# Three output projections as 64-row tiles, two blocks of tokens side by side

## The chip, the cores and the metric

The kernel runs on one core of a Trainium2 chip. The metric is device time in microseconds (us), lower is better. Engines: PE is TensorE (PEld its weight loads), DVE is VectorE, ACT is ScalarE, POOL is GpSimd, SP is SyncE, which here issues all DMAs.

## The reference

One transformer block in float32 on 2048 tokens of width 448: attention with 16 query heads of 28 and one key and value head, then a gated feed-forward of width 1792, each behind a layer norm and with a residual.

```python
x = A_x
h = x + _A_ref(_layernorm(x, axis=-1), A_wq, A_wk, A_wv, A_wo)
h2 = h + _B_ref(_layernorm(h, axis=-1), B_w1, B_w3, B_w2)
return h2
```

`_A_ref` ends with `o @ wo`, where `o` is the 2048 x 448 attention output and `wo` is 448 x 448. This last product is what the change touches.

## The kernel before

**Precision.** A float32 operand is split into a high part (float32r, 0) and a low part (1); a product is high x high + high x low + low x high. The attention output of a tile, transposed, is held as `OS[0]` and `OS[1]`, the weight as `WO[0]` and `WO[1]`. The 448 inputs are three chunks of 128 rows and one of 64. Both 64-row halves of chunk 3 of `OS` hold the same rows; in `WO[0]` rows 0 to 63 of chunk 3 are the high part and rows 64 to 127 the low part, so that one 128-row product gives two terms. A block of 128 tokens thus takes 3 x 3 + 2 = 11 matmuls (`mm_D`).

**Tiling.** The tokens are four tiles (t) of 512, each of four blocks (n) of 128. The attention of a tile is four groups of four heads (`NG`), a group 16 steps of 128 keys. A step is: scores transposed in three 32-row matmuls a head (L407), an exponential on ACT (L414), and the values product of all four heads (L423). Beside them, for groups that come later, run the score matmuls that find each row's maximum (L323, "units"), reduced on DVE (L333, L351) or by way of ACT (L344, L358, L364).

**Order.** All queues are written out by hand. The list `EVERY` sets the order of score matmuls (`H`), units (`U`, `D`, `S`, `E`, `R`) and values (`pv1`) on TensorE; it repeats every four steps. Other work is tied to a step: `at(s, fn)` puts `fn` into the instruction streams when step s is reached. Each engine takes its instructions in the order in which they are written; waits between engines are semaphores, put in where data or a buffer require it.

**The projection.** After step 14 of the first group of the next tile, the output of the tile that is done is projected: `wo_rows(t, n)` (11 full matmuls into one bank, then an add to the residual `X[t]` on DVE, L476) for n = 0 to 3. This happens for tiles 0, 1 and 2 within the attention; tile 3 is projected early in the feed-forward, in the same way. Between the blocks' projections stands other work on the same step: the layer norm statistics of blocks 0 to 2 (`ln_stats`: L195 and L196 on DVE), and in the stages of tiles 1 and 2 two normalizations of tile 0 (`ln_norm`: L211 on ACT) with their transposes and DMAs (`blocks`: L225 on DVE, L231 on SP). In the stages of tiles 1 and 2 the statistics of one earlier block stand ahead of the first projection.

**Banks.** PSUM has eight banks. One holds the values product, seven are dealt out by `bank()`, which takes the bank that a model of the engines (`Clock`) expects to be free first; `done()` gives it back.

**Half mode.** The feed-forward already has a scheme for 64-row tiles: `two` writes two lists of matmuls by turns, one on rows 0 to 63 and one on rows 64 to 127, into two banks; then the halves change banks. Before they do, `settle`, a one-element ACT read of one of the banks (L1028), orders the two halves' writes to a bank.

Of the kernel before, what the change touches and what calls it, by code (L numbers as in the profile page):

```python
# [10 lines left out]
AF = mybir.ActivationFunctionType  # L11
ALU = mybir.AluOpType
# [4 lines left out]
P = 128  # L17
S = 2048
D = 448
# [5 lines left out]
NQ = T // P  # L25
# [10 lines left out]
def block_kernel(  # L36
# [13 lines left out]
    ve, se, ge, pe, sy = nc.vector, nc.scalar, nc.gpsimd, nc.tensor, nc.sync  # L50
# [4 lines left out]
    def f(ap):  # L55
        return ap.bitcast(F32)
# [10 lines left out]
    X = [keep.tile([P, NQ, D], F32, name=f"X{t}") for t in range(NT)]  # L67
    ident = keep.tile([P, P], F32, name="ident")
    NEG = [keep.tile([P, 32], F32R, name=f"neg{k}") for k in range(2)]
    pexp = keep.tile([P, 32], F32, name="pexp")  # L70
# [3 lines left out]
    WO = [keep.tile([P, NG, D], F32R, name=f"WO{k}", tag=f"wo{k}") for k in range(2)]  # L74
    OT = keep.tile([P, NG, T], F32, name="OT")
    OS = [keep.tile([P, NG, T], F32R, name=f"OS{k}", tag=f"os{k}") for k in range(2)]
# [7 lines left out]
    def qs_tile():  # L84
        k, n_qs[0] = homes[n_qs[0] % len(homes)], n_qs[0] + 1
        return keep.tile([P, 2, T], F32R, name="qs", tag=f"q{k}")
# [52 lines left out]
    clock, ready = Clock(), {}  # L139
# [3 lines left out]
    def bank(name="pb"):  # L143
        k = min(free, key=lambda k: order[k])
        free.remove(k)
        if k < 7:
            ps = ps_w.tile([P, T], F32, name=name, tag=f"bank{k}")
        else:
            ps = ps_o.tile([P, T], F32, name="po")
        used[id(ps)] = ps, k  # L150
        ready.pop(id(ps), None)
        return ps

    def done(ps, at=None):
        k = used.pop(id(ps))[1]
        order[k] = ready.get(id(ps), clock.end) + 0.7 if at is None else at
        free.append(k)
# [155 lines left out]
    class Unit:  # L313
# [22 lines left out]
        def plain(self):  # L336
            self.ps = self.mm()
            self.red()
# [133 lines left out]
    def wo_rows(t, n):  # L472
# [3 lines left out]
        ve.tensor_tensor(X[t][:, n], ps, X[t][:, n], op=ALU.add)  # L476
        done(po)

    def split_w(k):
        wh, wl = [qs_tile().rearrange("p a (c m e) -> p (a c) m e", c=2, m=2)  # L480
                  for b in range(2)]
        ve.tensor_copy(wh, W13[k])
        ge.tensor_tensor(wl, W13[k], f(wh), op=ALU.subtract)
        return wh, wl
# [25 lines left out]
    with tc.tile_pool(name="start", bufs=1) as sp:  # L510
# [37 lines left out]
        def split_wo(c):  # L548
            ge.tensor_copy(WO[0][:, c], wo_r[:, c])
            r, k = (slice(0, P), 1) if c < 3 else (slice(64, P), 0)  # L550
            ge.tensor_tensor(WO[k][r, c], wo_r[r, c], f(WO[0][r, c]), op=ALU.subtract)

        def stats(t, *ns):
            for n in ns:
                ln_stats(t, n)
# [51 lines left out]
        def diffs(i, kt, n):  # L607
            us = HV[i, kt, n] = [[Unit(i, 2 * h + k, n, kt) for k in range(2)] for h in range(2)]
            return [(both_diff, u) for u in us]

        def sums(i, kt, n):
            return [(both_sum, u) for u in HV.pop((i, kt, n))]
# [4 lines left out]
        first = plain(0, 0, 0) + plain(0, 0, 1) + diffs(0, 0, 2) + plain(0, 1, 1) + sums(0, 0, 2) + plain(0, 1, 0) + diffs(0, 0, 3) + sums(0, 0, 3) + diffs(1, 0, 0) + sums(1, 0, 0) + plain(0, 2, 0) + plain(0, 2, 2) + plain(0, 2, 1) + plain(0, 3, 2) + plain(0, 3, 0) + diffs(0, 2, 3) + sums(0, 2, 3) + plain(0, 3, 1) + [(max_done, 0)] + diffs(1, 2, 0) + [(max_rows, 0), (max_out, 0)] + sums(1, 2, 0)  # L617
# [212 lines left out]
    def at(s, fn, *args):  # L830
        todo.setdefault(s, []).append((fn, args))

    for g in range(NG):
        at(1 + 2 * g, split_wo, g)
# [3 lines left out]
    for i in range(NI - 1):  # L838
        e = NC * (i + 1)
# [3 lines left out]
    for t in range(NT - 1):  # L843
        e = NC * NG * (t + 1)


        if t == 1:
            at(e + 14.7, ln_stats, 0, NQ - 1)
            at(e + 14.7, ln_rstd, 0)
        for n in range(NQ):  # L850
            at(e + 14.7, wo_rows, t, n)
            for m in {(1, 1): (0,), (1, 2): (1,), (2, 0): (2, 3)}.get((t, n), ()):
                at(e + 14.7, ln_norm, 0, m, True)
                at(e + 14.7, blocks, 0, m)
            if t == 0 and n == NQ - 1:
                continue
            late = NC * NG * (t + 2) + 14 if t < 2 else LAST - 12
            at(e + 14.7 if n < NQ - 1 else late + 0.7, ln_stats, t, n)
        if t:
            at(late + 2, ln_rstd, t)  # L860
            if t == 2:
                at(e + 18, fetch, 0)
# [15 lines left out]
    for s in range(AHEAD, LAST):  # L878
        i, c = divmod(s, NC)
        n, kt = divmod(c, NQ)  # L880
# [7 lines left out]
    units = [0] + [64 - 4 * (AHEAD - NC)] + [64] * (NI - 2)  # L888
# [98 lines left out]
    while n_pv[0] < LAST:  # L987
        for x in "H2 H0 H2 H1 H3 H0 H2 H1 H0 H3 H2 H0 H3 H1 H2 pv1 H2 H0 H1 H3 H2 H0 H1 H3 H2 H0 H1 H3 pv1 H2 H3 H1 H0 H2 H3 H1 H0 H2 H3 H1 H0 pv1 H1 H0 H2 H3 H1 H0 H3 H1 pv1 H3".split():
            if x != "pv1":
                score(int(x[1]))  # L990
                continue
            s = n_pv[0] + LAG
            if not values():
                continue
            if n_pv[0] in (LAST - 5, LAST - 2):
                WH[0, (n_pv[0] - LAST + 5) // 3] = split_w((n_pv[0] - LAST + 5) // 3)
            if n_pv[0] == LAST - 1:
                WS[0, 0] = split_w2(0)
            run(s + 0.4)
            run(s + 0.5)  # L1000
            run(s + 0.7)
            run(s)
# [8 lines left out]
    free.append(7)  # L1011
    order[7] = clock.end + 4

    HALF = (slice(0, 64), slice(64, 128))
    PAIRS3 = ((0, 0), (1, 0), (0, 1))
    FULL = 4
    def put_xd(t):
        XD[t] = wk_pool.tile([P, T], F32R, name="rb")
        se.activation(XD[t][:64], f(XT[t][2][64:, 3]), AF.Copy)

    def two(pairs):
        for units in zip(*pairs):
            for h, (ps, lhs, rhs, first, last) in enumerate(units):
                pe.matmul(ps[:, : rhs.shape[-1]], lhs, rhs, start=bool(first), stop=bool(last), skip_group_check=True)  # L1024
                clock.mm("half", h, ps, 0.016 + rhs.shape[-1] / 2400, first)

    def settle(ps):
        se.activation(pexp[:1, 8:9], ps[:1, :1], AF.Copy)  # L1028

    def hidden(t, k, ps, then=None):  # L1030
        sg = f(pt_ring()[:, 0])
# [17 lines left out]
    def products(t, W, m, h):  # L1049
        r = HALF[h]  # L1050
        u = [(W[b][r, c, 1 - m], XT[t][a][r, c]) for a, b in PAIRS3 for c in range(3)]
        return u + [(W[0][r, 3, 1 - m], XT[t][2][r, 3])]

    def ffn1_half(t, k, W, ps, late):
        us = [products(t, W, late, 0), products(t, W, 1 - late, 1)]
        if not late:
            us[0].append((W[1][HALF[0], 3, 1], XD[t][HALF[0]]))
            us[1].append((W[1][HALF[1], 3, 0], XT[t][2][HALF[1], 3]))
        to = (ps[0], ps[1]) if not late else (ps[1], ps[0])
        two([[(to[h], *u, not late and x == 0, late and x == len(us[h]) - 1) for x, u in enumerate(us[h])]  # L1060
             for h in range(2)])
        if not late:
            settle(ps[1])

    def ffn2(t, k, n):
        if n == 0 and k == 0:
            Y[t] = [bank() for _ in range(NQ)]
        hid, w2s = HID[t, k], WS[t, k]
        for m, (a, b) in enumerate(PAIRS3):
            pe.matmul(Y[t][n][:, :D], hid[a][:, n * P : (n + 1) * P], w2s[:, b],  # L1070
                      start=(k == 0 and m == 0), stop=(k == NF - 1 and m == 2), skip_group_check=True)

    def ffn2_half(t, k, late):
        if k == 0 and not late:
            Y[t] = [bank() for _ in range(NQ)]
        hid, w2s = HID[t, k], WS[t, k]
        us = [[], []]
        for h in range(2):
            for n0 in (2, 0) if late else (0, 2):
                n, r = n0 + (h ^ late), HALF[h]  # L1080
                for m, (a, b) in enumerate(PAIRS3):
                    us[h].append((Y[t][n], hid[a][r, n * P : (n + 1) * P], w2s[r, b],
                                  not late and k == 0 and m == 0, late and k == NF - 1 and m == 2))
        two(us)
        settle(Y[t][0 if late else 3])
# [47 lines left out]
    for t in range(NT):  # L1133
        for k in range(NF):
            end = t == tl and k >= NF - 2
            t2, k2 = divmod(NF * t + k + 2, NF)
            if t2 < NT:
                WH[t2, k2] = split_w(k2)
# [7 lines left out]
            else:  # L1146
                ps = [bank("pa"), bank("pa")]
# [54 lines left out]
```

## Time and profile before

| | us |
|---|---|
| median of 3 runs | 1160.41 (1159.94 to 1161.62) |
| the profiled execution, its own time | 1160.38 |
| its span | 1158.6 |
| projection of tile 0 (44 matmuls), start to the next score matmul | 280.36 to 289.65 |
| projection of tile 1 | 448.35 to 457.45 |
| projection of tile 2 | 615.89 to 625.00 |

Start times are from the first instruction of the span. A busy PE overlaps matmuls and isn't PE at its peak. In the timeline a row is a run of like instructions: start, length, engine, line, operation, output<-input, shapes, count, and in brackets the idle time before it with what ended it. The granted TensorE clock was 1.00 over the whole span. From about 30 to 738 us it is the attention, then the feed-forward.

### The profile page before, as it was taken

To read this page: it belongs to the slowest core of one execution; us is meant where nothing else is said; L and a number is where in the kernel's file an instruction comes from. 1 tells how busy PE (TensorE), PEld (TensorE's weight loads), DVE (VectorE), ACT (ScalarE), POOL (GpSimd) and SP (SyncE) were. 2 spreads that over 40 slices of the span, in tenths; PEclk is the share of its full clock that TensorE was granted. 3 is DMA by queue.
4 is the path that set the end of the run, shared out by engine and by line. 5 is a ranking of instruction groups with operands and counts; after the bars stand their busy time and mean duration, and the time that the engine had idled before them with its cause. 6 is when DMAs were issued, how large, how long until landed. Compare 5 with 4: busy or idle time off the path is not lost.

```text
span 1158.6 us, 25640 instructions
## 1 busy us (share of the span) xinstructions
PE 1149.0 (99%) x10154; PEld 772.7 (67%) x10154; DVE 805.8 (70%) x1498; ACT 764.3 (66%) x1587; POOL 330.2 (29%) x242
## 2 busy tenths in 40 slices
PE   8999999999999999999999999999999999999998
PEld 6664444446444445444445444589999999999997
DVE  8878999897999998999988983163543444344333
ACT  5649999997999997999997999512222222222221
POOL 5312001101101111110111011345565556556552
PEclk9999999999999999999999999999999999999999
DMA  4010100001000002000012100143211101000000
GB/s 168 10 38 1 34 13 18 19 15 47 19 12 10 19 24 54 19 20 3 19 24 55 50 19 14 56 103 96 73 39 20 41 1 49 17 33 33 1 1 33
DMA packets 66680, 38.15 MB, mean 33 GB/s; under 512 B 41728, under 2 KB 59392, under 8 KB 66560
## 3 DMA queue, kind: packets, MB, share of 16 engines
q1 hardware_dynamic: 66560, 36.51, 11.5%
q8 instruction: 79, 1.29, 0.5%
q14 instruction: 41, 0.34, 0.1%
HBM read 24.04 MB, written 7.47 MB: 27 GB/s over the span
## 4 chain that ended last, share of the span: by engine, by line
PE 94%; ACT 2%; DVE 2%; issue 1%; DMA 1%; SPq 0%; POOL 0%; ACTq 0%; POOLq 0%
PE po L423 21%; PE pb L407 20%; PE pa L1024 18%; PE pa L323 10%; PE pb L1024 9%; PE pa L166 5%; PE pb L166 4%; PE po L1024 4%; PE pb L1070 1%; ACT OT L430 1%; ACT ab L344 1%; DVE mx L333 1%; PE pb L273 0%; ACT pt L414 0%; PE po L166 0%
## 5 line engine op out<-in xcount | busy, mean ns | idle before, releaser
L333 DVE TENSOR_REDUCE mx<-pa 128x1 f32<-128x512 f32 x689 | 440.1, 685 | 22.1 <-PE pb L407 13.0
L407 PE MATMUL pb<-qs,KS 32*128 32x512 f32 x3072 | 384.9, 425 | 0.0
L414 ACT ACTIVATE pt<-pb 128x512 f32<-128x512 f32 x684 | 365.9, 621 | 20.1 <-PE pb L407 17.3
L407 PEld LDWEIGHTS pb<-qs,KS 32*128 32x128 f32 x3072 | 234.0, 182 | 132.2 <-ACT pt L414 66.9
L323 PE MATMUL pa<-KS,qs 32*128 32x512 f32 x886 | 311.7, 459 | 1.3
L1024 PE MATMUL pa<-xl,qs 64*128 64x512 f32 x1044 | 195.4, 388 | 0.0
L323 PEld LDWEIGHTS pa<-KS,qs 32*128 32x128 f32 x886 | 138.6, 182 | 83.6 <-DVE mx L333 46.3
L423 PE MATMUL po<-pt,VA 128*32 128x512 f32 x1368 | 182.2, 605 | 0.4 <-ACT pt L414 0.4
L1024 PE MATMUL pa<-xh,qs 64*128 64x512 f32 x739 | 159.9, 388 | 0.0
L454 POOL TENSOR_TENSOR OT<-OT,rb 128x512 f32<-128x512 f32 x15 | 19.7, 1311 | 458.1 <-DMA rb<-sd 240.9
L1024 PE MATMUL pb<-w2s,pt 64*128 64x448 f32 x1050 | 145.2, 360 | 0.0
L1034 DVE TENSOR_TENSOR pt<-pa,pt 128x512 f32<-128x512 f32 x49 | 33.8, 691 | 159.0 <-ACT pt L1032 152.9
L1024 PEld LDWEIGHTS pa<-xl,qs 64*128 64x128 f32 x1044 | 141.9, 184 | 3.1
L1024 PEld LDWEIGHTS pb<-w2s,pt 64*128 64x128 f32 x1050 | 125.2, 184 | 2.0 <-DVE pt L1040 0.2
L351 DVE CUSTOM_DVE_ANT_0 ab<-pa,ab 128x512 f32<-128x512 f32 x138 | 93.6, 686 | 39.5 <-PE pa L323 28.4
L1024 PEld LDWEIGHTS pa<-xh,qs 64*128 64x128 f32 x739 | 108.4, 184 | 3.2
L414 ACT ACTIVATE xl<-pb 128x512 f32<-128x512 f32 x170 | 99.6, 610 | 8.9 <-PE pb L407 6.8
L414 ACT ACTIVATE xh<-pb 128x512 f32<-128x512 f32 x170 | 104.5, 633 | 0.0
L1032 ACT ACTIVATE pt<-pa 128x512 f32<-128x512 f32 x49 | 29.3, 597 | 94.7 <-PE pa L1024 90.9
L423 PE MATMUL po<-xl,VA 128*32 128x512 f32 x340 | 89.4, 605 | 0.0
L423 PE MATMUL po<-xh,VA 128*32 128x512 f32 x340 | 89.4, 605 | 0.0
L344 ACT ACTIVATE ab<-pa 128x512 f32<-128x512 f32 x138 | 82.2, 608 | 6.7 <-PE pa L323 4.9
(156 smaller groups left out, 1411.4 us busy)
## 6 DMA issues: line engine op xcount, KB each, us to landing
rb<-sd SPq DMA_DIRECT2D x64, 64.0 KB
xr<-xn SPq DMA_DIRECT2D x64, 56.0 KB
QR<-OT SPq DMA_DIRECT2D x60, 56.0 KB
QR<-in_B_w_dram SPq DMA_DIRECT2D x16, 192.0 KB
xh<-xr SPq DMA_DIRECT2D x4, 768.0 KB
X<-in_A_x_dram SPq DMA_DIRECT2D x3, 896.0 KB
out_dram<-X SPq DMA_DIRECT2D x3, 896.0 KB
w<-in_B_w_dram SPq DMA_DIRECT2D x8, 192.0 KB
```

Source lines behind the costliest of these rows:

```text
L166: pe.matmul(ps, lhs[b][:, cb, lsl], (rhs[2] if ca == 3 and len(rhs) == 3 else rhs[a])[:, ca, rsl], start=(k == 0), stop=(k == len(terms) - 1),
L323: pe.matmul(ps, QS[i][r, 0, n * P : (n + 1) * P], KS[0][r, kt * T : (kt + 1) * T] if keys is None else keys[r], start=True, stop=True)
L333: ve.tensor_reduce(self.to(), ps, axis=AX.X, op=ALU.max)
L344: se.activation(self.ab, ps, AF.Relu)
L351: ve.tensor_tensor_reduce(self.ab, ps, self.ab, 1.0, -3.0e38, ALU.add, ALU.max, self.to())
L407: pe.matmul(self.ps, KS[k % 2][r, c * P : (c + 1) * P], QS[i][r, k // 2], start=(k == 0), stop=(k == 2))
L414: se.activation(f(PT[i, c, p][:, jj]), self.ps, AF.Exp, bias=0.0, scale=SCALE)
L423: pe.matmul(PO[i][32 * j : 32 * j + 32], VA[:, c], f(PT[i, c, j // 2][:, j % 2]), start=(c == 0), stop=(c == NC - 1))
L454: eng.tensor_tensor(o, o, rb, op=ALU.mult)
L1024: pe.matmul(ps[:, : rhs.shape[-1]], lhs, rhs, start=bool(first), stop=bool(last), skip_group_check=True)
L1032: se.activation(sg, ps[0], AF.Silu)
L1034: ve.tensor_tensor(sg, ps[1], sg, op=ALU.mult)
```

## The change

The projections of tiles 0, 1 and 2 become one call, `wo_all(t)`, at the place where `wo_rows(t, 0)` stood; tile 3 keeps `wo_rows`. `wo_all` takes four banks, one for each block, and fills them in four parts. In an early part one half of the rows works on block n and the other on block n + 1; in the late part of the same two blocks the halves have changed places. An early part has 11 pairs of matmuls, a late one 10. The odd term of chunk 3 (low part of o with high part of w) is now a 64-row product of its own; for it rows 64 to 127 of `WO[1]`, chunk 3, are filled with a copy of the weight. The order of parts is: early for blocks 0 and 1, early for 2 and 3, late for 0 and 1, two adds, late for 2 and 3, two adds. Statistics, normalizations and transposes that stood between the blocks keep their order among themselves and come behind the whole call.

```diff
+    def wo_part(ps, n, late):
+        us = [[], []]
+        for h in range(2):
+            m, r = n + (h ^ late), HALF[h]
+            sl = slice(m * P, (m + 1) * P)
+            terms = [(a, b, c) for a, b in PAIRS3 for c in range(3)] + [(0, 0, 3)]
+            if not late:
+                terms.append((h, 1, 3))
+            for x, (a, b, c) in enumerate(terms):
+                us[h].append((ps[m], OS[b][r, c, sl], WO[a][r, c], not late and x == 0, late and x == len(terms) - 1))
+        two(us)
+        if not late:
+            settle(ps[n + 1])
+
+    def wo_all(t):
+        ps = [bank("pa") for n in range(NQ)]
+        wo_part(ps, 0, 0)
+        wo_part(ps, 2, 0)
+        for n in (0, 2):
+            wo_part(ps, n, 1)
+            for m in (n, n + 1):
+                ve.tensor_tensor(X[t][:, m], ps[m][:, :D], X[t][:, m], op=ALU.add)
+                done(ps[m])
...
             ge.tensor_tensor(WO[k][r, c], wo_r[r, c], f(WO[0][r, c]), op=ALU.subtract)
+            if c == 3:
+                ge.tensor_copy(WO[1][r, c], wo_r[r, c])
...
         for n in range(NQ):
-            at(e + 14.7, wo_rows, t, n)
+            if n == 0:
+                at(e + 14.7, wo_all, t)
             for m in {(1, 1): (0,), (1, 2): (1,), (2, 0): (2, 3)}.get((t, n), ()):
                 at(e + 14.7, ln_norm, 0, m, True)
                 at(e + 14.7, blocks, 0, m)
```

`HALF`, `PAIRS3`, `two` and `settle` are moved up unchanged, so lines behind them have other numbers: the add is L500, the matmuls are L509, the settling read is L513.

The order on DVE at the projection of tile 0 (X_77 is tile 0 of the residual; st and mv are statistics; pa is a bank; - is before, + is the change):

```order
-L476 TENSOR_TENSOR X_77<-pa,X_77 128x448
+L500 TENSOR_TENSOR X_77<-pa,X_77 128x448 x4
 L195 BN_STATS st<-X_77 128x6
 L196 BN_AGGR mv<-st 128x2
-L476 TENSOR_TENSOR X_77<-pa,X_77 128x448
 L195 BN_STATS st<-X_77 128x6
 L196 BN_AGGR mv<-st 128x2
-L476 TENSOR_TENSOR X_77<-pa,X_77 128x448
 L195 BN_STATS st<-X_77 128x6
 L196 BN_AGGR mv<-st 128x2
-L476 TENSOR_TENSOR X_77<-pa,X_77 128x448
 L351 ISA ab,mx_97<-pa,ab 128x512
```

Four adds now stand ahead of the three pairs of statistics; before, the last add stood behind them and directly ahead of L351, the first score reduction after the stage.

The order on DVE at the projection of tile 1, from the first statistics of tile 1 (X_78) on (xn holds a normalized block of tile 0):

```order
-L476 TENSOR_TENSOR X_78<-pa,X_78 128x448
 L225 STREAM_TRANSPOSE xn<-xn 128x448
 L195 BN_STATS st<-X_78 128x6
 L196 BN_AGGR mv<-st 128x2
-L476 TENSOR_TENSOR X_78<-pa,X_78 128x448
 L225 STREAM_TRANSPOSE xn<-xn 128x448
 L195 BN_STATS st<-X_78 128x6
 L196 BN_AGGR mv<-st 128x2
-L476 TENSOR_TENSOR X_78<-pa,X_78 128x448
 L351 ISA ab,mx_97<-pa,ab 128x512
```

Here two transposes stand with the statistics between the adds and L351. At tile 2 it is the same, with both transposes ahead of the statistics.

The order on TensorE at tile 0, where the second early part ends and the first late part begins (pa_4118 to pa_4121 are the banks' tiles of blocks 0 to 3):

```order
L509 MATMUL pa_4120<-WO0_92,OS0_95 128x448
L509 MATMUL pa_4121<-WO0_92,OS0_95 128x448
L509 MATMUL pa_4120<-WO0_92,OS1_96 128x448
L509 MATMUL pa_4121<-WO1_93,OS1_96 128x448
L509 MATMUL pa_4119<-WO0_92,OS0_95 128x448
L509 MATMUL pa_4118<-WO0_92,OS0_95 128x448
```

The halves have changed places: the first of a pair, on rows 0 to 63, went to block 2 and now goes to block 1. Behind the call the order on TensorE is the old one.

More of the change, by code (lines that the diff above doesn't have):

```diff
@@ L477, in wo_rows, with two, settle @@
         done(po)
+    def wo_part(ps, n, late):
[20 more added lines that the diff above has]
+                done(ps[m])
+    HALF = (slice(0, 64), slice(64, 128))
+    PAIRS3 = ((0, 0), (1, 0), (0, 1))
+    def two(pairs):
+        for units in zip(*pairs):
+            for h, (ps, lhs, rhs, first, last) in enumerate(units):
+                pe.matmul(ps[:, : rhs.shape[-1]], lhs, rhs, start=bool(first), stop=bool(last), skip_group_check=True)
+                clock.mm("half", h, ps, 0.016 + rhs.shape[-1] / 2400, first)
+    def settle(ps):
+        se.activation(pexp[:1, 8:9], ps[:1, :1], AF.Copy)
     def split_w(k):
@@ L1012, in block_kernel @@
     order[7] = clock.end + 4
-    HALF = (slice(0, 64), slice(64, 128))
-    PAIRS3 = ((0, 0), (1, 0), (0, 1))
     FULL = 4
@@ L1019, in put_xd @@
         se.activation(XD[t][:64], f(XT[t][2][64:, 3]), AF.Copy)
[L1021 to L1028, printed above, removed]
     def hidden(t, k, ps, then=None):
```

## The prediction

> **What bounds the kernel now.** I read the engine table first, then the chain of waits, then the timeline around the three places that the change touches.
>
> The engine table (engine, busy us, share of the span, instructions):
>
> ```profile
> PE 1149.0 (99%) x10154; PEld 772.7 (67%) x10154; DVE 805.8 (70%) x1498; ACT 764.3 (66%) x1587; POOL 330.2 (29%) x242
> ```
>
> TensorE is called busy throughout, but matmuls overlap in it, and DVE and ACT at 70% and 66% are means over an attention phase and a feed-forward phase. So the chain of waits decides: start, length, engine and line, first around the projection of tile 0, then around that of tile 2.
>
> ```profile
> 280.44 9.30 PE pa L166 x44
> ...
> 289.76 0.63 DVE X L476
> 290.38 0.60 DVE ab L351
> ...
> 290.99 3.09 DVE mx L333 x5
> ```
>
> ```profile
> 615.96 9.13 PE pa L166 x44
> ...
> 625.11 0.63 DVE X L476
> 625.74 0.60 DVE ab L351
> ```
>
> The 44 matmuls bound their stage. What then comes last isn't TensorE: it is DVE's last add (L476), the score reduction behind it (L351), and five more reductions (L333). Whatever DVE does between the last add and L351 is on the path. The same place in the timeline (start, length, engine, line, operation, idle time before it and what ended it):
>
> ```profile
> 280.36 8.97 PEld L166 LDWEIGHTS pa<-WO,OS 128*128 128x128 f32 x44 [0.84 <-ACT pt L414]
> 283.60 0.63 DVE L195 BATCH_NORM_STATS2 st<-X 128x6 f32<-128x448 f32 x1
> 284.26 0.18 DVE L196 BATCH_NORM_AGGREGATE mv<-st 128x2 f32<-128x6 f32 x1
> 289.65 0.18 PEld L407 LDWEIGHTS pb<-qs,KS 32*128 32x128 f32 x2 [0.31 <-issue]
> 289.76 0.63 DVE L476 TENSOR_TENSOR X<-pa,X 128x448 f32<-128x448 f32 x1 [0.77 <-PE pa L166]
> 290.30 0.68 DVE L351 CUSTOM_DVE_ANT_0 ab<-pa,ab 128x512 f32<-128x512 f32 x1
> 290.70 1.58 ACT L414 ACTIVATE pt<-pb 128x512 f32<-128x512 f32 x3 [9.38 <-PE pb L407]
> 290.90 3.16 DVE L333 TENSOR_REDUCE mx<-pa 128x1 f32<-128x512 f32 x5
> 292.24 0.59 PE L323 MATMUL pa<-KS,qs 32*128 32x512 f32 x2
> ```
>
> The reader should see three things. The statistics (L195, L196) run inside the stage, in gaps in which DVE waits for TensorE anyway: they are free. ACT idles 9.38 us there. And the second of the five reductions ends at 290.90 + 2 x 3.16 / 5 = 292.16; TensorE's next score matmuls start at 292.24, 0.08 us later, since they take the banks that the reductions release. DVE has no slack there.
>
> The stage of tile 1 reads the same way:
>
> ```profile
> 448.35 8.80 PEld L166 LDWEIGHTS pa<-WO,OS 128*128 128x128 f32 x44 [0.84 <-ACT pt L414]
> 457.56 0.62 DVE L476 TENSOR_TENSOR X<-pa,X 128x448 f32<-128x448 f32 x1 [0.33 <-PE pa L166]
> 458.11 0.68 DVE L351 CUSTOM_DVE_ANT_0 ab<-pa,ab 128x512 f32<-128x512 f32 x1
> 458.71 3.16 DVE L333 TENSOR_REDUCE mx<-pa 128x1 f32<-128x512 f32 x5
> 460.05 0.59 PE L323 MATMUL pa<-KS,qs 32*128 32x512 f32 x2
> ```
>
> Its second reduction ends at 458.71 + 1.26 = 459.97, and TensorE goes on at 460.05: again 0.08 us.
>
> **The change, part by part.**
>
> *Matmuls.* A stage had 44 steps of 128 rows; it gets 42 steps of two 64-row matmuls side by side (11 + 11 + 10 + 10). What a step takes is in the feed-forward, where both kinds run on 448 columns:
>
> ```profile
> 764.20 2.39 PE L166 MATMUL po<-WO,OS 128*128 128x448 f32 x11
> 766.42 2.40 PE L166 MATMUL pa<-WO,OS 128*128 128x448 f32 x11
> ...
> 785.47 1.37 PE L1024 MATMUL pb<-w2s,pt 64*128 64x448 f32 x12
> 786.67 0.86 PE L1024 MATMUL pa<-xl,qs 64*128 64x512 f32 x6
> ```
>
> Full: (766.42 - 764.20) / 11 = 0.202 us. Pairs: (786.67 - 785.47) / 6 = 0.200 us. So 44 x 0.202 - 42 x 0.200 = 0.48 us less in each stage. Both kinds change the tiling after the 32-row score matmuls, so I leave the 0.84 us ahead of the stage and the 0.31 us behind it as they are.
>
> *Adds.* Before, three of the four adds were over when the last matmul ended. Now the third and the fourth wait for the last pair: the third starts 0.48 us earlier than the last one did, and the fourth 0.54 us behind it (the distance of L476 to L351 at 289.76 and 290.30). The last add starts 0.06 us later than before.
>
> *Statistics and transposes.* This is the term that counts. The order on DVE now has all four adds ahead of the statistics, so three pairs of L195 and L196, and in the later two stages two transposes (L225), stand between the last add and L351. Their lengths in a row, from the stage of tile 2:
>
> ```profile
> 615.89 8.81 PEld L166 LDWEIGHTS pa<-WO,OS 128*128 128x128 f32 x44 [0.84 <-ACT xl L414]
> 618.96 1.16 DVE L225 STREAM_TRANSPOSE xn<-xn 128x448 f32<-128x448 f32 x2
> 620.05 0.58 DVE L195 BATCH_NORM_STATS2 st<-X 128x6 f32<-128x448 f32 x1
> 620.77 0.59 DVE L476 TENSOR_TENSOR X<-pa,X 128x448 f32<-128x448 f32 x1
> ...
> 625.65 0.68 DVE L351 CUSTOM_DVE_ANT_0 ab<-pa,ab 128x512 f32<-128x512 f32 x1
> ```
>
> A pair takes 620.77 - 620.05 = 0.72 us, two transposes 620.05 - 618.96 = 1.09 us. Three pairs: 2.16 us. L351 shifts by 0.06 + 2.16 = 2.22 us in the first stage and by 0.06 + 2.16 + 1.09 = 3.31 us in each of the other two. The gaps that held this work stay, but empty: the adds that open them now come at the end. What is late next is TensorE, which needs the reductions' banks (0.08 us of slack, above), and through it ACT, the values matmuls and all that follows.
>
> *Settling reads.* Two one-element ACT instructions a stage; a late part waits for the first or the second of them.
>
> ```profile
> L1028 ACT ACTIVATE pexp<-pa 1x1 f32<-1x1 f32 x43 | 6.9, 160 | 76.0 <-PE pa L1024 76.0
> L549 POOL CAST WO<-OT 128x448 fp32r<-128x448 f32 x4 | 2.2, 561 | 7.1 <-DMA OT<-in_A_wo_dram 7.1
> ```
>
> One takes 0.16 us on an ACT that is idle; between it and the late part lie 11 steps on the other two banks (2.2 us). So 0; without that cover each of the six would hold TensorE for its 0.16 us at least, some 1 us in all. The extra cast of 64 rows takes about the 0.56 us of L549, once, early, on a POOL that is idle 71% of the time: 0.
>
> *Queues.* The transposes' DMAs leave SP later, and the loads and the sums' DMAs (L437) stand behind them:
>
> ```profile
> 454.31 4.09 SPq L231 DMA_DIRECT2D xr<-xn  x8
> ...
> 462.56 2.47 SPq L437 DMA_DIRECT2D sm<-OT  x4
> 467.72 0.24 DVE L444 RECIPROCAL sm<-sm 128x16 f32<-128x16 f32 x1
> ```
>
> In tile 1 the two transposes would end some 11.2 and 12.5 us after the stage's start (9.3 for the last add, 0.54, then pairs and transposes by turns); 4.09 us of DMAs issued from 11.3 on, then six loads (3.4 us, the time from 458.5 to 461.9), end near 18.8. L437 stood at 14.2 and with the shift wants 17.5. It can be 1.3 us late. Before, the reciprocal came without waiting 2.69 us after the last of these was issued (462.56 + 2.47 to 467.72), so between 0 and 1.3 us reach DVE. I take 0, which is what the row shows, and keep 1.3 for the range.
>
> *Sum.* 2.22 + 3.31 + 3.31 = 8.84 us, with TensorE's 0.48 us already in it. On the profiled execution's 1160.38 us this gives **1169.2 us**. The median of the runs is 1160.41 us, so nothing has to be corrected.
>
> *Its bounds.* Upwards: if the pairs run at what the stage itself needed (no gain), 3 x 0.48 = 1.4 us, and SP's 1.3 us: 1171.9 us. Downwards: ACT's first exponentials come 0.48 us earlier, which may return up to 0.3 us a stage (an estimate: less than the 0.48): 1168.3 us.
>
> **The rivals.**
>
> *Half is given back.* DVE is not full in the long stretches between stages, and TensorE might catch up. For: DVE's reductions wait a little for TensorE there. Against: ACT hardly does. Its whole waiting from 295 to 448 us (who waited for whom, us, times, longest) is
>
> ```profile
> ACT xl L414 <- PE pa L323: 0.4, 1, 0.4
> ```
>
> An engine that never waits can't catch up. Half of 8.84 us would give 1164.8 us.
>
> *Enough free banks (not slower).* Place: the score matmuls after the stage. If TensorE didn't need the banks of the late reductions before its next idle time, only the saved steps would remain: 1160.38 - 3 x 0.48 = 1158.9 us. It decides from the point at which more than 3.3 us of slack lies between a reduction and the matmul on its bank. The rows show 0.08 us in two stages, the chain runs through DVE, and two banks, not one, now come free only after the last matmul of the stage.
>
> *Only the adds crowd.* Were the statistics and transposes still hidden, L351 would shift by 0.06 us a stage: 1160.6 us. The Trainium skill, in TensorEngine Tiling (Array Packing), section PSUM Bottleneck, says that tiling speeds up TensorE but not the copying out of PSUM, which may become the bottleneck; by that rule alone the time would be this one. The trace agrees as to the adds, but the order puts far more than adds behind the stage.
>
> *The pairs don't run side by side* (the change would not do what it says). 84 x 0.202 = 17.0 us in place of 8.9, three times, on top of the sum: 1169.2 + 3 x 8.5 = about 1195 us. The rows at 785.47 speak against it.
>
> **How the numbers follow.** Forecast 0.78; half given back 0.10; free banks 0.05; only adds 0.05; not side by side 0.02. About 0.2% (2.3 us) is what a measurement of this kernel can tell from no change; so slower is 0.78 + 0.10 + 0.02 = 0.90, and the remaining 0.10 is two cases within 0.2%, of which I give 0.02 to faster, since 1158.9 lies near that edge. The range goes from the half case, 1164.8, to the upper bound, 1171.9, and leaves out 0.12 by the cases.
>
> **What would show it.** Right: 84 matmuls in 8.8 us or so in each stage; four adds in a row's place with the last at the end; L351 about 12.2 us after the first stage's start and 13.0 us after the others' (before: 9.94, 9.76, 9.76); TensorE's pair of L323 matmuls later by the same 2.2 and 3.3 us; the chain naming L195 and L225. Wrong: an unchanged L323 with a later L351 (free banks); stages of 17 us; a second wait at L444; or the distance from one stage to the next shrinking by what was lost (given back).

## The result and the profile after

| | before | after |
|---|---|---|
| median of 6 runs, us | 1160.51 (1159.71 to 1161.62) | 1174.30 (1171.91 to 1179.35) |
| the profiled execution, its own time | 1160.38 | 1178.54 |
| its span | 1158.6 | 1176.7 |
| its mean granted TensorE clock | 1.000 | 0.988 |

The ratio is 1.0125, 95% interval 1.0113 to 1.0137: the change costs 13.8 us. The forecast was 1169.2 us, with a range from 1164.8 to 1171.9: the direction was right, and the time lies above the range.

The timeline around the projection of tile 0, after the change (start, length, engine, line, operation, idle time before it and what ended it):

```profile
283.03 8.94 PE L509 MATMUL pa<-WO,OS 64*128 64x448 f32 x84
285.61 0.16 ACT L513 ACTIVATE pexp<-pa 1x1 f32<-1x1 f32 x1 [1.60 <-PE pa L509]
289.94 1.16 DVE L500 TENSOR_TENSOR X<-pa,X 128x448 f32<-128x448 f32 x2 [6.70 <-PE pa L509]
291.91 0.49 PE L323 MATMUL pa<-KS,qs 32*128 32x512 f32 x1
292.01 1.15 DVE L500 TENSOR_TENSOR X<-pa,X 128x448 f32<-128x448 f32 x2 [0.91 <-PE pa L509]
293.08 0.62 DVE L195 BATCH_NORM_STATS2 st<-X 128x6 f32<-128x448 f32 x1
293.83 0.59 DVE L195 BATCH_NORM_STATS2 st<-X 128x6 f32<-128x448 f32 x1
294.56 0.59 DVE L195 BATCH_NORM_STATS2 st<-X 128x6 f32<-128x448 f32 x1
295.29 0.66 DVE L351 CUSTOM_DVE_ANT_0 ab<-pa,ab 128x512 f32<-128x512 f32 x1
296.01 0.49 PE L323 MATMUL pa<-KD,qs 32*128 32x512 f32 x1 [0.87 <-DVE mx L351]
297.21 0.50 PE L323 MATMUL pa<-KS,qs 32*128 32x512 f32 x2
```

The reader should see that the pairs do run side by side (84 matmuls in 8.94 us) and that the next score matmul starts 8.88 us after the stage's start, where it was some 9.3: 0.42 us earlier. And DVE, which used to go from the last add straight to L351, now works through three statistics first. L351 starts 12.26 us after the stage's start, not 9.94, and TensorE stands waiting for it.

The chain of waits of the same execution now goes through that work (start, length, engine, line):

```profile
283.10 8.88 PE pa L509 x84
291.99 0.02 issue
292.01 1.15 DVE X L500 x2
293.17 0.55 DVE st L195
...
294.64 0.52 DVE st L195
...
295.37 0.57 DVE ab L351
```

Two rows of the stage of tile 1, and then the stage of tile 2; in both, two transposes stand in the queue too:

```profile
453.74 8.78 PE L509 MATMUL pa<-WO,OS 64*128 64x448 f32 x84
...
466.89 0.66 DVE L351 CUSTOM_DVE_ANT_0 ab<-pa,ab 128x512 f32<-128x512 f32 x1
...
625.74 8.78 PE L509 MATMUL pa<-WO,OS 64*128 64x448 f32 x84
...
634.57 1.16 DVE L500 TENSOR_TENSOR X<-pa,X 128x448 f32<-128x448 f32 x2 [0.87 <-PE pa L509]
...
635.64 1.16 DVE L225 STREAM_TRANSPOSE xn<-xn 128x448 f32<-128x448 f32 x2
...
638.90 0.66 DVE L351 CUSTOM_DVE_ANT_0 ab<-pa,ab 128x512 f32<-128x512 f32 x1
...
639.62 0.79 PE L323 MATMUL pa<-KD,qs 32*128 32x512 f32 x1 [1.93 <-DVE mx L351]
640.22 0.79 PE L323 MATMUL pa<-KS,qs 32*128 32x512 f32 x1
```

Two things stand here. In the stage of tile 2 TensorE waits 1.93 us in one piece for L351. And behind the wait one score matmul takes 0.79 us, where the same line takes 0.49 us in the rows of tile 0 above. The windows say why (stretch, its length, busy time and instructions of PE, PEld, DVE, ACT, POOL, granted clock, DMA share, GB/s):

```profile
298.00:302.00 4.00, 4.00 (x31) 2.48 (x24) 2.70 (x6) 3.40 (x7) 0.00 (x0) 0.57 0.01 1
468.00:473.00 5.00, 4.90 (x35) 2.10 (x34) 3.43 (x8) 3.54 (x7) 0.00 (x0) 0.66 0.45 95
639.00:653.00 14.00, 13.38 (x75) 5.75 (x75) 9.12 (x19) 8.94 (x17) 3.03 (x4) 0.52 0.25 57
90.00:94.00 4.00, 4.00 (x30) 1.46 (x27) 1.77 (x3) 2.41 (x5) 3.84 (x5) 0.58 0.02 4
```

Right behind each of the three stages TensorE is granted half its clock for a while: 4.00 x (1 - 0.57) / 0.5 = 3.4 us, 5.00 x (1 - 0.66) / 0.5 = 3.4 us, and 14.00 x (1 - 0.52) / 0.5 = 13.4 us. The last window shows a fourth dip, at 90 us, and there is one of the same length from 8 to 12 us: both lie far ahead of the first changed stage.

The profiled execution is one of the two longest, and times go with the clock. The two longest after the change (1178.54 and 1179.35 us) have a mean clock of 0.988, two of the shorter ones (1172.71 and 1172.59 us) have 0.996. That is 6.3 us for 0.008; a straight line through them gives 1169.5 us at a clock of 1.000, and one through all six runs 1168.8 us (both are estimates). So I formed two theories. **Theory 1:** the order on DVE costs the forecast 8.8 us. **Theory 2:** the rest is the lower clock that follows TensorE's stall. The rival to both: the 64-row pairs themselves cost the time, or bring the clock down.

### The profile page after: what moved, and what is told of

It is laid out like the page before. It is cut to its first block, busy times and chain, and to the rows that moved or that the text cites. A ratio compares the mean times of both kernels' runs of the same rounds, so it can differ in the third digit from the quotient of the medians.

```text
span 1176.7 us, 25874 instructions
## 1 busy us (share of the span) xinstructions
PE 1160.7 (99%) x10274; PEld 777.1 (66%) x10274; DVE 804.6 (68%) x1498; ACT 767.1 (65%) x1593; POOL 330.4 (28%) x243
## 4 chain that ended last, share of the span: by engine, by line
PE 95%; DVE 2%; ACT 2%; issue 1%; DMA 0%; POOL 0%; ACTq 0%; POOLq 0%
PE po L423 22%; PE pa L509 20%; PE pb L407 20%; PE pa L323 11%; PE pb L509 9%; PE pb L166 4%; PE po L509 4%; PE pa L166 3%; PE pb L1098 1%; ACT ab L344 1%; ACT OT L430 0%; PE pb L273 0%; DVE st L195 0%; PE po L166 0%; ACT pt L414 0%
## 5 line engine op out<-in xcount | busy, mean ns | idle before, releaser
L407 PE MATMUL pb<-qs,KS 32*128 32x512 f32 x3072 | 391.2, 430 | 0.0
L407 PEld LDWEIGHTS pb<-qs,KS 32*128 32x128 f32 x3072 | 237.7, 185 | 133.3 <-ACT pt L414 67.2
L323 PE MATMUL pa<-KS,qs 32*128 32x512 f32 x886 | 315.3, 465 | 2.5 <-DVE X L500 1.1
L509 PE MATMUL pa<-xl,qs 64*128 64x512 f32 x1044 | 194.9, 388 | 0.0
L423 PE MATMUL po<-pt,VA 128*32 128x512 f32 x1368 | 185.2, 614 | 0.4 <-ACT pt L414 0.4
L509 PE MATMUL pa<-xh,qs 64*128 64x512 f32 x739 | 159.4, 388 | 0.0
L509 PE MATMUL pb<-w2s,pt 64*128 64x448 f32 x1050 | 145.4, 360 | 0.0
L509 PEld LDWEIGHTS pa<-xl,qs 64*128 64x128 f32 x1044 | 141.5, 184 | 3.2
L509 PEld LDWEIGHTS pb<-w2s,pt 64*128 64x128 f32 x1050 | 125.4, 184 | 2.0 <-DVE pt L1068 0.2
L351 DVE CUSTOM_DVE_ANT_0 ab<-pa,ab 128x512 f32<-128x512 f32 x138 | 93.5, 686 | 42.6 <-PE pa L323 32.7
L509 PEld LDWEIGHTS pa<-xh,qs 64*128 64x128 f32 x739 | 108.0, 184 | 3.3
```

Of the source, the lines that this page charges most:

```text
L323: pe.matmul(ps, QS[i][r, 0, n * P : (n + 1) * P], KS[0][r, kt * T : (kt + 1) * T] if keys is None else keys[r], start=True, stop=True)
L351: ve.tensor_tensor_reduce(self.ab, ps, self.ab, 1.0, -3.0e38, ALU.add, ALU.max, self.to())
L407: pe.matmul(self.ps, KS[k % 2][r, c * P : (c + 1) * P], QS[i][r, k // 2], start=(k == 0), stop=(k == 2))
L423: pe.matmul(PO[i][32 * j : 32 * j + 32], VA[:, c], f(PT[i, c, j // 2][:, j % 2]), start=(c == 0), stop=(c == NC - 1))
```

## The experiments

**The order without the pairs.** The kernel before, with its four full-row projections written ahead of everything else:

```diff
         for n in range(NQ):
             at(e + 14.7, wo_rows, t, n)
+        for n in range(NQ):
             for m in {(1, 1): (0,), (1, 2): (1,), (2, 0): (2, 3)}.get((t, n), ()):
```

> The full-row projections of the kernel before, all four written ahead of the statistics, normalizations and transposes, as in the change. Theory 1 (the time is lost by DVE's order, not by the 64-row pairs): L351 stands 2.16 us later behind the stage of tile 0 and 3.25 us later behind those of tiles 1 and 2, 8.66 us in all, so 1169.0 us with a full granted clock. Theory 2 (TensorE, stalled behind DVE, is then granted a lower clock): some 3 to 5 us more, up to 1174, with a mean granted clock of 0.99 and low windows right behind the stages. Rival (the 64-row pairs cost the time or the clock): 1160.4 us and a clock of 1.00.

Measured: 1173.97 us (1170.12 to 1175.85, 4 runs), ratio 1.0111 (1.0092 to 1.0131), clock 0.993 to 0.997 in all four. There isn't one 64-row pair in these stages, and the time of the change is there. Its stage of tile 1, first the timeline, then the windows of its stages of tiles 1 and 2:

```profile
459.34 0.62 DVE L476 TENSOR_TENSOR X<-pa,X 128x448 f32<-128x448 f32 x1 [1.61 <-PE pa L166]
...
463.14 0.66 DVE L351 CUSTOM_DVE_ANT_0 ab<-pa,ab 128x512 f32<-128x512 f32 x1
...
463.86 0.79 PE L323 MATMUL pa<-KD,qs 32*128 32x512 f32 x1 [2.24 <-DVE mx L351]
```

```profile
460.00:480.00 20.00, 17.76 (x115) 7.32 (x114) 13.87 (x29) 12.15 (x23) 0.00 (x0) 0.66 0.24 51
640.00:660.00 20.00, 19.93 (x184) 9.53 (x184) 17.04 (x34) 18.59 (x36) 4.32 (x5) 0.91 0.35 102
```

A wait of 2.24 us, then half the clock for 20.00 x 0.34 / 0.5 = 13.6 us, and behind the next stage for 3.6 us. The rival falls.

**The pairs without the order.** The changed kernel, but normalizations and transposes stand in DVE's gap ahead of the adds, and the statistics at the head of the next stage (those of tile 2 in the feed-forward):

```diff
         wo_part(ps, 2, 0)
+        for m in ((), (0, 1), (2, 3))[t]:
+            ln_norm(0, m, True)
+            blocks(0, m)
         for n in (0, 2):
...
+            for n in range(NQ):
+                at(e + 14.7, ln_stats, t - 1, n)
```

> The 64-row pairs of the change, but the normalizations and transposes stand on DVE ahead of the adds, and the statistics at the head of the next stage (those of tile 2 in the feed-forward): behind the stage DVE has the last add and then L351 at once. Theories 1 and 2: L351 0.06 us later a stage than in the kernel before, 1160.4 us within 1.5, granted clock 1.00. Rival (the 64-row pairs cost the time or the clock): 1168 us or more, with low windows of the clock behind the stages.

Measured: 1161.94 us (1161.02 to 1163.73, 10 runs), ratio 1.0012 (1.0003 to 1.0021), clock 1.000 in nine of ten. Its stage of tile 0:

```profile
280.19 8.78 PE L512 MATMUL pa<-WO,OS 64*128 64x448 f32 x84
...
289.02 1.16 DVE L503 TENSOR_TENSOR X<-pa,X 128x448 f32<-128x448 f32 x2 [0.87 <-PE pa L512]
290.09 0.68 DVE L351 CUSTOM_DVE_ANT_0 ab<-pa,ab 128x512 f32<-128x512 f32 x1
290.23 0.50 PE L323 MATMUL pa<-KS,qs 32*128 32x512 f32 x1 [0.36 <-DVE X L503]
```

L351 comes 9.90 us after the stage's start, and 9.89 us in the other two stages (before: 9.94, 9.76 and 9.76). So 12.4 of the 13.8 us are gone. The 1.4 us that remain lie just outside what was expected (1160.4 within 1.5), and far from the rival's 1168.

**Part of the order taken back.** The changed kernel with only the normalizations and their transposes moved to the end of the early parts, ahead of all four adds, as in the first lines of the diff above; the statistics stay behind the adds.

> The changed kernel with the transposes on DVE ahead of the adds; the statistics stay behind them. Theory 1: L351 2.22 us later in each of the three stages, 6.7 us in all, so 1167.0 us at a full clock: 2.2 us less than the order of the change costs. Theory 2: with shorter stalls behind the stages of tiles 1 and 2 the low clock is shorter or gone there, so 1167 to 1170. Rival (the pairs cost the time): 1172 to 1174, as the change.

Measured: 1169.80 us (1169.07 to 1173.65, 4 runs), ratio 1.0086 (1.0069 to 1.0103), clock 0.992 to 0.997. That is 4.5 us less than the change, of which the transposes' place makes 2.2 by theory 1; windows of 1 us show 3.4 us of half clock behind each of the last two stages. Both theories agree with that, and the rival doesn't: the pairs are all still there.

**TensorE kept busy in its stall.** The changed kernel, with matmuls that nobody reads put behind each stage, at the first score matmul after the first values product: once 5, 9 and 9 of the 32-row score matmuls, once 6, 11 and 11 full ones. DVE's order is the change's.

```diff
             if k == 0:
                 self.ps = bank()
+            if k == 0 and fill[0] == 2:
+                fill[0] = 0
+                for _ in range(fill[1]):
+                    pe.matmul(self.ps[:, :D], OS[0][:, 0, :P], WO[0][:, 0], start=True, stop=True)
```

> The changed kernel with 5, 9 and 9 repeats of the first score matmul behind the three stages, into a bank that TensorE holds already, while DVE works off its queue; the first score matmul that counts overwrites them, so the output is the same. DVE's order is that of the change. Theory 2 (the rest beyond 8.84 us is the clock after TensorE's stall): the clock stays at 1.00 behind the stages and the time is 1169 us within 1.5. Rival (the low clock comes from the 64-row pairs, or the rest isn't the clock): it stays at 1172 to 1178 with low windows. If 32-row matmuls don't count as work for the clock, the same: then the clock windows are low in spite of a short stall.

> The changed kernel with 6, 11 and 11 matmuls of 128 rows and 448 columns behind the three stages (some 1.2 and 2.2 us), in place of the 32-row fillers, into a bank that TensorE holds already and whose content is overwritten. DVE's order is that of the change. Two of the four runs with 32-row fillers had a clock of 0.99 still. Theory 2 with the addition that a 32-row matmul keeps the clock less well than a full one: nearly all runs at a clock of 1.00 and 1169.2 us within 1.5. Rival (the fillers' kind doesn't matter; what remains of the stall, or its place, brings the low clock): again about half of the runs at 0.99 and 1172 to 1176 us, the median above 1170.5.

Measured with 32-row fillers: 1171.22 us (1169.42 to 1175.61, 4 runs), ratio 1.0102 (1.0078 to 1.0127). Two runs had a clock of 1.000 (1170.14 and 1169.42 us), two had 0.991 and 0.994 (1175.61 and 1172.29 us). With full fillers: **1169.40 us** (1168.16 to 1173.39, 6 runs), ratio 1.0078 (1.0063 to 1.0094), clock 0.999 or 1.000 in five of six; the sixth, 0.996, is the 1173.39. The stage of tile 1 with full fillers, and its window:

```profile
461.63 1.06 PE L427 MATMUL po<-pt,VA 128*32 128x512 f32 x8
462.63 2.49 PE L410 MATMUL pb<-WO,OS 128*128 128x448 f32 x11
...
465.06 0.49 PE L323 MATMUL pa<-KD,qs 32*128 32x512 f32 x1
```

```profile
460.00:480.00 20.00, 19.45 (x167) 9.52 (x167) 18.18 (x37) 15.20 (x30) 0.00 (x0) 1.00 0.27 62
```

TensorE did more work than in the changed kernel, L351 came as late (12.27, 13.16 and 13.32 us after the stages' starts), and the kernel became 4.9 us faster. That is theory 2: the clock, not the late L351 alone, made the rest. Whether 32-row fillers keep the clock less well than full ones is left open by two low runs of four against one of six.

**A shorter stall.** The kernel before, with the statistics of one block computed twice more between the last add and L351 (2 x 0.72 us):

```diff
+        for x in range(2):
+            at(e + 14.7, ln_stats, t, 1)
         if t:
             at(late + 2, ln_rstd, t)
```

> The kernel before, with the statistics of one block computed twice more between the last add and L351 in each of the three stages: 2 x 0.72 = 1.44 us of DVE work. Output the same. Theory 1: L351 1.44 us later a stage, 4.3 us in all: 1164.8 us. Theory 2 (the clock drops after TensorE's stall) in two forms: if any stall does it, the clock falls below 1.00 and the time is 1166 us or more; if it takes a long one, as behind the 2.2 and 3.3 us of the change, the clock stays at 1.00 and the time is 1164.8 us within 0.7. Rival (no stall, but the pairs): 1164.8 us too, with a clock of 1.00, but that rival has fallen already with the full-row kernel in the order of the change, at 1174 us.

Measured: 1167.24 us (1166.05 to 1167.74, 4 runs), ratio 1.0057 (1.0043 to 1.0071), clock 0.997 to 0.999. L351 came 11.38 us after the first stage's start, 1.44 later than before, which looks as foreseen; but the matmuls of that stage had taken 0.17 us longer in the kernel before. From the last add to L351 it is 2.17 us in each of the three stages, where it was 0.54 or 0.55, so the work added some 1.6 us a stage, 4.9 us in all, not 4.3. The time rose by 6.9 us, 2.0 more than that. The timeline behind the stage of tile 2 and its window:

```profile
628.28 0.63 DVE L476 TENSOR_TENSOR X<-pa,X 128x448 f32<-128x448 f32 x1 [0.77 <-PE pa L166]
...
630.06 0.50 PE L407 MATMUL pb<-qs,KS 32*128 32x512 f32 x1
...
630.45 0.66 DVE L351 CUSTOM_DVE_ANT_0 ab<-pa,ab 128x512 f32<-128x512 f32 x1
...
631.17 0.49 PE L323 MATMUL pa<-KD,qs 32*128 32x512 f32 x1 [0.61 <-DVE mx L351]
...
632.80 1.67 PE L423 MATMUL po<-pt,VA 128*32 128x512 f32 x8
634.39 0.79 PE L323 MATMUL pa<-KD,qs 32*128 32x512 f32 x1
```

```profile
620.00:640.00 20.00, 19.29 (x132) 12.36 (x135) 15.26 (x33) 9.98 (x19) 3.04 (x4) 0.91 0.28 64
```

So the form "only a long stall" falls: a wait of 0.61 us was followed by 3.6 us of half clock here. The other two stages of this run have the same wait of 0.61 us and no half clock behind it.

**What the pairs can bring.** Two kernels with the pairs and nothing but adds at the stage's end: one with the statistics of tile 2 in the last group of the attention and not in the feed-forward, and on top of it one in which the last add of a stage goes by way of ACT and POOL. A third is the kernel before with only its last add moved in that way.

```diff
-                ve.tensor_tensor(X[t][:, m], ps[m][:, :D], X[t][:, m], op=ALU.add)
+                y, eng = ps[m][:, :D], ve
+                if m == 3:
+                    y, eng = ln_pool.tile([P, 512], F32, name="xn", bufs=4)[:, :D], ge
+                    se.activation(y, ps[m][:, :D], AF.Copy)
+                eng.tensor_tensor(X[t][:, m], y, X[t][:, m], op=ALU.add)
```

> As e2, but the statistics of tile 2 stand in the last group of the attention, where DVE is idle, and not in the feed-forward. Theory (the 1.4 us that e2 stood above the kernel before come from the work put into the feed-forward, not from the pairs): 1160.5 us within 0.8, granted clock 1.00. Rival (the pairs themselves cost them): 1161.9 us.

> As e6 (pairs, with normalizations, transposes and statistics away from the stage's end), and of the two last adds of a stage one goes another way: ACT, idle there, copies the bank to SBUF and POOL adds the copy. DVE then has one add in place of two between the last pair and L351. Theory (DVE's queue behind the stage sets what follows): L351 0.54 us earlier than in e6 in each stage, and since TensorE comes back 0.4 us earlier than in the kernel before, 0.3 to 0.5 us a stage are gained: 1159 us, from 1158.7 to 1159.7, clock 1.00. Rival (something else behind the stage, ACT or the score matmuls, takes its place): as e6 within 0.5 us.

> The kernel before, with only the last add of each of the three stages by way of ACT (copy) and POOL (add). L351 can start 0.5 us earlier. Theory (DVE's queue behind the stage sets what follows, here too): TensorE's wait for the reductions, some 0.3 us a stage, goes: 1159.5 us, from 1159.0 to 1160.0. Rival (TensorE's own work behind the stage is as long): 1160.5 us.

| kernel | median, us (11 runs) | ratio, 95% |
|---|---|---|
| pairs, statistics late | 1161.06 | 1.0006 (0.9997 to 1.0015) |
| the same, last add by ACT and POOL | **1159.10** | 0.9988 (0.9980 to 0.9997) |
| full rows, last add by ACT and POOL | 1160.96 | 1.0005 (0.9996 to 1.0014) |

The kernel before stood at 1160.35 us (27 runs) beside them. The first can't be told from it. Its excess is 0.7 us, where that of the kernel with the statistics in the feed-forward was 1.4; this fits the theory that the work put into the feed-forward cost a part, but the two intervals overlap, so it isn't shown. The second is faster than the kernel before and the changed one. Its stage of tile 0, and then the full-row kernel's L351:

```profile
280.33 8.94 PE L516 MATMUL pa<-WO,OS 64*128 64x448 f32 x84
...
289.14 0.55 ACT L506 ACTIVATE xn<-pa 128x448 f32<-128x448 f32 x1 [3.74 <-PE pa L516]
...
289.31 0.63 DVE L507 TENSOR_TENSOR X<-pa,X 128x448 f32<-128x448 f32 x1 [0.91 <-PE pa L516]
...
289.76 1.15 POOL L507 TENSOR_TENSOR X<-xn,X 128x448 f32<-128x448 f32 x1 [21.70 <-ACT xn L506]
289.85 0.68 DVE L351 CUSTOM_DVE_ANT_0 ab<-pa,ab 128x512 f32<-128x512 f32 x1
```

```profile
289.89 0.69 DVE L351 CUSTOM_DVE_ANT_0 ab<-pa,ab 128x512 f32<-128x512 f32 x1 [1.22 <-PE pa L323]
```

With pairs L351 starts 9.52, 9.55 and 9.39 us after the three stages' starts, 0.42, 0.21 and 0.37 earlier than before: 1.0 of the 1.25 us gained. With full rows the same move leaves DVE idle for 1.22 us, waiting for TensorE; L351 starts 9.70 to 9.72 us after the starts, 0.3 us earlier in all three together, and nothing is gained: the expected 1159.5 us was a miss. Here the pairs' shorter stage is worth something only when DVE's tail is short, and a shorter tail only with the pairs. The Trainium skill, in TensorEngine Tiling (Array Packing), section PSUM Bottleneck, advises to use both ScalarE and VectorE to copy out of PSUM once tiling has sped up TensorE; the second row of the table agrees, by 2.0 us against the first.

## Why the prediction was right and wrong

Point by point:

- **Matmuls**, -0.48 us a stage: 0.42 measured in the first stage (score matmuls resume after 8.88 us, 9.30 before, when they started at 289.66), 0.40 in the others (8.70 and 8.71 us, 9.11 before). The pairs do lie side by side.
- **Adds**, 0.06 us: some 0.1. From the first statistics behind the adds (293.08) to L351 it is 2.21 us; the rest of L351's shift in the first stage, 2.32 us, is the adds'.
- **Statistics and transposes**, L351 later by 2.22, 3.31 and 3.31 us: 295.29 - 283.03 = 12.26 us after the stage's start in the first stage, 13.15 and 13.16 in the others (12.2, 13.0 and 13.0 forecast), so 2.32, 3.39 and 3.40 us. Shown as a cause by the order without the pairs, and by the pairs without the order.
- **Settling reads and the cast**, 0: the reads take 0.16 us on an idle ACT, as the row at 285.61 shows, and the two fastest versions that keep both take 1161.06 and 1159.10 us, against 1160.35 before.
- **SP's queue**, 0 to 1.3 us: the reciprocal (L444) behind the stage of tile 1 waited 0.29 us for its DMA.
- **Half is given back**: hardly. The distance from one stage's start to the next's, and from the last one's to the span's end, in the kernel with full fillers (clock 1.00) is 169.74, 171.21 and 545.82 us, before it was 167.99, 167.54 and 542.71: 8.5 us more, where L351's shifts in that kernel add up to 9.3.
- **The pairs don't run side by side**: they do, as the stages of 8.94 and 8.78 us show. That rival's price has a slip: 17.0 - 8.9 is 8.1 us a stage and not 8.5, so its time would have been about 1193.5 us.

So the sum of 8.84 us was right for a TensorE at full clock: 8.5 us by these distances, and a median of 1169.40 us against a forecast of 1169.2.

The step that failed is the one that asked what is late next. The prediction answered that it is TensorE, and through it ACT, the values matmuls and all that follows, and let them be late by DVE's shift only; the durations behind the stall were taken to be those of before, so its sum has no term for a lower clock. The runs show that a TensorE left idle in the stall worked at half clock for a while behind it: the three distances of the changed kernel's profiled execution are 170.71, 172.00 and 550.96 us, 6.9 us more in all than with the fillers, and those stretches hold 3.4 + 3.4 + 13.4 us of half clock behind the stages. Another 2.7 us of that execution lie ahead of the first stage, where the dips at 8 and at 90 us are. The granted clock of 1.00 over the whole span of the kernel before was carried over to a kernel in which TensorE waits up to 1.93 us in one piece.

By the Trainium skill, TensorE: Matmul & The Clock Gate, section Part 1: The HAM clock gate, TensorE falls to half rate after an idle window of about 3.4 us that runs freely. The low stretches here agree as to the length, 3.4 us or four times that, and as to the chance in it. They don't agree as to the idle time that it takes: half clock followed waits of 1.93 us and of 0.61 us.

## What to carry to other kernels

When a change pulls work together into one call, look at what used to stand between its pieces: here it was free in the gaps, and behind the call it stood in the one queue that everything waited for. Price a new wait of TensorE higher than its length: half clock can follow it, at random. Here 20.2 us of half clock came with 6.9 us of time, some 0.34 us for each (an estimate from two executions). Other work for TensorE in the wait avoided it in five runs of six. And the faster matmul stage paid here only when the last copy out of its banks was shared among the engines that were idle.

## What the hardware showed that was not expected

In the profiled executions, half-clock stretches came in two lengths only. Read in windows of 1 us they are 3.4 us, or 13.6 to 13.7 us, four times as long (the 3.6 and 13.4 us above are the same stretches in coarser windows); one more is cut off by the end of its execution. They follow a stall by chance. With L351 2.2 to 3.4 us late, every run of the change, of the order alone and of the kernel with the transposes ahead lost clock (0.988 to 0.997). With L351 1.6 us late, three runs of four were below 0.999, and the fourth, at 0.999, is the profiled one with its short dip: a single short dip hardly shows in the mean. With L351 in its old place, the kernel before was below 0.999 in two of the 51 runs that stood beside the experiments (both 0.997, at 1162.35 and 1163.62 us).

So a dip comes now and then without any of these stalls. The one at 90 us did: TensorE has no wait between 80 us and that dip. What sets a dip off, and why it sometimes lasts four times as long, these runs don't settle.
